# Layer B with VectorE 32x32 transposes, softmax weights normalised ahead of the value product, and column-tiled masks and sums

## The chip, the cores and the metric

The kernel runs on one core of a Trainium2 chip. The metric is the device time of one execution in microseconds (us), as a median over several runs. A core has TensorE (PE in the profile; PEld is its weight load), VectorE (DVE), ScalarE (ACT), GpSimd (POOL) and SyncE (SP), which here issues the transfers. In this program each engine executes its instructions in the order in which they are written, and waits for the others through semaphores.

## The reference, cut

Four layers, A, B, A, B, each on the layernorm of a residual stream of 2048 tokens x 640. The change touches B alone, which is recurrent: 64 segments of 32 tokens, each preceded by 8 memory rows that the segment before it has put out.

```python
def _B_ref(x, mem0, Wq, Wk, Wv, Wo, seg_len):      # H = 32 heads, Dh = 128, M = 8, seg_len = 32
    ...
    for s in range(n_seg):                          # 64 segments, one after the other
        h = concatenate([mem, x[:, s*32:(s+1)*32]]) # 8 + 32 rows
        q, k, v = h @ Wq, h @ Wk, h @ Wv
        scores = where(mask, q @ k.T * scale, -1e9)
        o = softmax(scores) @ v @ Wo
        mem = o[:, :M]                              # the next segment needs these
        outs.append(o[:, M:])
```

Two layers of 64 segments make 128 segments in a row, so a microsecond in a segment is 128 us of the total.

## The kernel before: the parts that matter

A projection ("thin" matmul) has 32 token columns as its stationary operand. Four such matmuls run side by side in the array as column tiles of 32, each with 512 columns of the weights. Q and K come out with tokens on the partitions, but the scores need the head dimension there. The kernel before evicts them to SBUF, lets TensorE transpose them (four 128x128 blocks) and scatters the result.

```python
def thin_parts(cols, Wt, b, name):
    ps = ps_tile([128, 512], F32, name)                    # one PSUM bank
    def part(c):
        for j in range(4):
            n = 4 * b + j
            nc.tensor.matmul(ps[32*j:32*j+32, :], lhsT=cols(c), rhs=Wt[:, c, 512*n:512*n+512],
                             start=(c == 0), stop=(c == NCH-1), tile_position=(0, 32*j), ...)
    return ps, [lambda c=c: part(c) for c in range(NCH)]   # NCH = 5, so 20 matmuls
def transp4(sb_half, name):
    tp = ps_tile([128, 4, 128], BF16, name)
    for i in range(4):
        nc.tensor.transpose(tp[:, i, :], sb_half[:, 128*i:128*i+128], C.identb[:])
    return tp
# ... scores(b): the mask is added by one full-array matmul of 320 columns, then 32 small column-tiled ones, then Exp
# ... sums(b): row-tiled matmuls with ones; values(b): row-tiled; both into the OTL tiles
def inverse(b, jp):                                        # 1/sum as exp(-ln(sum)), 320 columns, on ScalarE
    R = ...; nc.scalar.activation(out=R[:], in_=OTL[b, jp][:, :, 1, 0:160], func=ACT.Ln)
    nc.scalar.activation(out=R[:], in_=R[:], func=ACT.Exp, scale=-1.0)
def scale(b, jp):                                          # the heads' outputs are normalised AFTER the value product
    nc.vector.tensor_tensor(out=OTsb[...], in0=OTL[b, jp][:, :, 0, 0:160], in1=R[:], op=ALU.mult)
    for i in range(2):
        nc.gpsimd.tensor_tensor(out=Rtot[:], in0=Rtot[:], in1=R[:, i], op=ALU.add)   # range check
# ... one segment, in the order of the program:
Qa = thin_mm(cols, W.wq, 0, "b_Qa"); evac("act", Qsb[:, 0, :], Qa[:], SCB)
Ka = thin_mm(cols, W.wk, 0, "b_Ka"); evac("dve", Ksb[:, 0, :], Ka[:])
Qb = thin_mm(cols, W.wq, 1, "b_Qb"); evac("act", Qsb[:, 1, :], Qb[:], SCB)
TPQa = transp4(Qsb[:, 0, :], "b_TPQ"); scatter(...); TPKa = transp4(Ksb[:, 0, :], "b_TPK"); scatter(...)
# ... V, scores, sums, values, inverse, scale for both halves; OPS: 64 output matmuls;
# fill(): projections of later tokens ("tail") or the output pass of postponed rows ("OPSd") in TensorE's gaps
msb = ...; nc.scalar.copy(msb[:], ops[:])                  # memory rows: eviction, then six selecting matmuls (b_MT)
nc.tensor.matmul(mt[:, 0, :], lhsT=msb[:, 0:128], rhs=selm[:, 0, :], ...)                 # x6
```

PSUM, TensorE's output memory, is used up in this program: four tiles of one bank (`ps_tile`) and two of two banks (`pot`, for the heads' outputs). All engines are held to the program's order.

Of the kernel before, what the change touches and what calls it, by code (L numbers as in the profile page):

```python
# [28 lines left out]
D = 640  # L29
# [29 lines left out]
def layernorm_tile(nc, pool, C, xt, xn_out, name):  # L59
    stats = pool.tile([128, 2, nc.vector.BN_STATS_DIM], F32, name=f"{name}_st", tag="ln_st")  # L60
    nc.vector.bn_stats(out=stats[:, 0, :], in_=xt[:, 0:320])
    nc.vector.bn_stats(out=stats[:, 1, :], in_=xt[:, 320:640])
    mv = pool.tile([128, nc.vector.BN_AGGR_DIM], F32, name=f"{name}_mv", tag="ln_mv")
    nc.vector.bn_aggr(out=mv[:], in_=stats[:])
    rstd = pool.tile([128, 1], F32, name=f"{name}_rstd", tag="ln_rstd")
    nc.vector.tensor_scalar(out=rstd[:], in0=mv[:, 1:2], scalar1=LN_EPS, scalar2=None, op0=ALU.add)
    nc.gpsimd.tensor_tensor(out=rstd[:], in0=rstd[:], in1=C.mhalf[:, 0:1], op=ALU.pow)
    nc.vector.tensor_scalar(out=xn_out, in0=xt, scalar1=mv[:, 0:1], scalar2=rstd[:, 0:1],
                            op0=ALU.subtract, op1=ALU.mult)
# [496 lines left out]
def load_B_weights(nc, tc, ctx, B_Wq, B_Wk, B_Wv):  # L566
# [4 lines left out]
    for nm, src in (("wq", B_Wq), ("wk", B_Wk), ("wv", B_Wv)):  # L571
        t = wp.tile([128, NCH, 4096], BF16, name=f"b_{nm}")
        setattr(W, nm, t)
        sv = src.rearrange("(c p) h e -> p c (h e)", p=128)
        for c in range(NCH):
            loads.append(lambda t=t, sv=sv, c=c: nc.sync.dma_start(t[:, c, :], sv[:, c, :]))
# [3 lines left out]
def layer_B(nc, tc, C, W, wo_src, x_src, xb_src, x_dst, mem0, general, nsteps=64, out_bf16=False):  # L580





# [6 lines left out]
    with ExitStack() as ctx:  # L592
# [12 lines left out]
        selm = st.tile([128, 2, 8], BF16, name="b_sel")  # L605
        nc.vector.tensor_tensor(out=selm[:, 0, :], in0=C.identb[:, 24:32], in1=C.identb[:, 88:96], op=ALU.add)
        nc.vector.tensor_tensor(out=selm[:, 1, :], in0=C.identb[:, 56:64], in1=C.identb[:, 120:128], op=ALU.add)
        ones = st.tile([128, 128], BF16, name="b_ones")
        nc.vector.memset(ones[:], 1.0)
        if not general:  # L610
            Rtot = st.tile([128, 160], BF16, name="b_Rtot")
            nc.vector.memset(Rtot[:], 0.0)
        XO = st.tile([64, 320], F32, name="b_XO")
        nc.vector.memset(XO[:], 0.0)
        negs = wk.tile([128, 32], F32, name="b_negs", tag="Qsb")
        nc.vector.memset(negs[:], -1e9)
        mask = st.tile([128, 2, 40], BF16, name="b_mask")
        maskf = wk.tile([128, 2, 40], F32, name="b_maskf", tag="Ksb")
        nc.vector.memset(maskf[:], 0.0)
        for j in range(4):  # L620
            r0 = 32 * j
            nc.gpsimd.affine_select(out=maskf[r0:r0 + 24, 0, 0:24], in_=negs[r0:r0 + 24, 0:24],
                                    pattern=[[-1, 24]], compare_op=ALU.is_gt, fill=0.0, base=0, channel_multiplier=1)
            nc.vector.memset(maskf[r0:r0 + 8, 1, 0:24], -1e9)
            nc.gpsimd.affine_select(out=maskf[r0:r0 + 8, 1, 32:40], in_=negs[r0:r0 + 8, 0:8],
                                    pattern=[[-1, 8]], compare_op=ALU.is_gt, fill=0.0, base=0, channel_multiplier=1)
        nc.vector.tensor_copy(mask[:], maskf[:])
        if general:
            maskq = st.tile([128, 40], BF16, name="b_maskq")
            maskqf = wk.tile([128, 40], F32, name="b_maskqf", tag="Vsb")  # L630
# [8 lines left out]
        def evac(eng, dst, src, scale=None):  # L639
            if eng == "act":  # L640
                if scale is None:
                    nc.scalar.copy(dst, src)
                else:
                    nc.scalar.activation(out=dst, in_=src, func=ACT.Copy, scale=scale)
            else:
                if scale is None:
                    nc.vector.tensor_copy(dst, src)
                else:
                    nc.vector.tensor_scalar(out=dst, in0=src, scalar1=scale, scalar2=None, op0=ALU.mult)

# [10 lines left out]
        def ln_norm(g):  # L661
            xt = ln_x.pop(g)
            layernorm_tile(nc, sm, C, xt[:], xt[:], "b_ln")
            ln_n[g] = xt
# [33 lines left out]
        def thin_parts(cols, Wt, b, name):  # L698
            ps = ps_tile([128, 512], F32, name)

            def part(c):
                for j in range(4):
                    n = 4 * b + j
                    nc.tensor.matmul(ps[32 * j:32 * j + 32, :], lhsT=cols(c), rhs=Wt[:, c, 512 * n:512 * n + 512],
                                     start=(c == 0), stop=(c == NCH - 1), tile_position=(0, 32 * j), skip_group_check=True)
            return ps, [lambda c=c: part(c) for c in range(NCH)]

        def thin_mm(cols, Wt, b, name):
            ps, parts = thin_parts(cols, Wt, b, name)
            for f in parts:  # L710
                f()
            return ps

        def transp4(sb_half, name):
            tp = ps_tile([128, 4, 128], BF16, name)
            for i in range(4):
                nc.tensor.transpose(tp[:, i, :], sb_half[:, 128 * i:128 * i + 128], C.identb[:])
            return tp

        def scatter(eng, tp, b, dst3, t0, t1, c0):  # L720
            src = tp[:].rearrange("p i (j t) -> p i j t", j=4)[:, :, :, t0:t1]
            dst = dst3[:, 16 * b:16 * b + 16, c0:c0 + (t1 - t0)].rearrange("p (j i) c -> p i j c", j=4)
            evac(eng, dst, src)


        QTt, KTt, Vtb, Vt, tail_sb = {}, {}, {}, {}, {}
# [10 lines left out]
        class TailUnit:  # L737


            def __init__(self, T, kind, b, eng):  # L740
                self.T, self.kind, self.b, self.eng = T, kind, b, eng
                self.parts = None

            def start(self):
                Wt = {"Q": W.wq, "K": W.wk, "V": W.wv}[self.kind]
                self.ps, self.parts = thin_parts(tail_cols(self.T), Wt, self.b, "b_tail")
                if self.b == 0:
                    if self.kind == "V":
                        Vtb[self.T] = wk2.tile([128, 2, 512], BF16, name="b_Vtb", tag="Vtb")
                    else:  # L750
                        self.sb2 = tail_sb[self.kind] = wk.tile([128, 2, 512], BF16, name="b_tsb", tag="Qsb")

            def run(self, k):
# [3 lines left out]
                while k > 0 and self.parts:  # L757
                    self.parts.pop(0)()
                    k -= 1
                    if not self.parts:  # L760
                        if self.kind == "V":
                            evac(self.eng, Vtb[self.T][:, self.b, :], self.ps[:])
                        else:
                            self.sb = tail_sb[self.kind][:, self.b, :]
                            evac(self.eng, self.sb, self.ps[:], SCB if self.kind == "Q" else None)
                return k

            def transposes(self):
                if self.kind != "V":
                    self.tp = transp4(self.sb, "b_ttp")  # L770

            def finish(self):
                if self.kind != "V":
                    d = QTt if self.kind == "Q" else KTt
                    if self.b == 0:
                        d[self.T] = wk.tile([128, 32, 32], BF16, name=f"b_{self.kind}Tt", tag=f"{self.kind}Tt")
                    scatter(self.eng, self.tp, self.b, d[self.T], 0, 32, 0)
# [30 lines left out]
        def add_out(ops, XO, name):  # L808

            nc.vector.tensor_tensor(out=XO[0:64, :], in0=ops[0:64, :], in1=XO[0:64, :], op=ALU.add)  # L810
            if out_bf16:
                xnb = wk.tile([64, 320], BF16, name=name, tag=name)
# [10 lines left out]
        m0 = wk.tile([8, D], BF16, name="b_m0", tag="OTsb")  # L823
        nc.sync.dma_start(m0[:], mem0)
# [3 lines left out]
        alloc_h(0)  # L828
        mt = ps_tile([128, NCH, 8], BF16, "b_m0T")
        for c in range(NCH):  # L830
            nc.tensor.transpose(mt[:, c, :], m0[0:8, 128 * c:128 * c + 128], C.identb[0:8, 0:8])
        nc.vector.tensor_copy(hT[0][:, :, 24:32], mt[:])
        alloc_qk(0)
        for kind in ("Q", "K", "V"):
            for b in range(2):
                u = TailUnit(0, kind, b, ("act", "dve")[b])
                u.run(NCH)
                u.transposes()
                u.finish()
        for nm, Wt, sc, dst in (("Q", W.wq, SCB, QT), ("K", W.wk, None, KT)):  # L840
            for b in range(2):
                ps = thin_mm(lambda c: hT[0][:, c, 0:32], Wt, b, "b_first")
                sb = wk.tile([128, 512], BF16, name="b_fsb", tag=("Qsb", "Ksb")[b])
                evac(("act", "dve")[b], sb[:], ps[:], sc)
                scatter(("act", "dve")[b], transp4(sb, "b_ttp"), b, heads(dst[0]), 0, 24, 0)
# [14 lines left out]
        for s in range(nsteps):  # L860
# [12 lines left out]
            elif T + 1 < NT:  # L873
                kind = " VQK"[i4]
                units = [TailUnit(T + 1, kind, 0, "act"), TailUnit(T + 1, kind, 1, "dve")]
# [8 lines left out]
            for u in units:  # L884
                if isinstance(u, TailUnit) and u.kind != "V":
                    queue.append((0.31, lambda u=u: (u.transposes(), u.finish())))
# [10 lines left out]
            Qsb = wk.tile([128, 2, 512], BF16, name="b_Qsb", tag="Qsb")  # L897
            Ksb = wk.tile([128, 2, 512], BF16, name="b_Ksb", tag="Ksb")
            Vsb = wk.tile([128, 2, 512], BF16, name="b_Vsb", tag="Vsb")
            PT = wk.tile([128, 2, 2, 4, 40], BF16, name="b_PT", tag="PT")  # L900
# [4 lines left out]
            mrows = []  # L905

            def row_max(b):
# [20 lines left out]
                mr = wk.tile([3, 16, 40], BF16, name="b_mrows", tag="mrows")  # L928
# [3 lines left out]

            def scores(b):
                sp = ps_tile([128, 2, 4, 40], F32, "b_SP")
                nc.tensor.matmul(sp[:], lhsT=C.identb[:], rhs=mask[:].unsqueeze(2).to_broadcast([128, 2, 4, 40]),
                                 start=True, stop=False, skip_group_check=True)
                for r in range(4):
                    for k, n in ((0, 32), (1, 8)):
                        for j in range(4):
                            h = 16 * b + 4 * j + r  # L940
                            nc.tensor.matmul(sp[32 * j:32 * j + n, k, r, :], lhsT=KT[s][:, 40 * h + 32 * k:40 * h + 32 * k + n],
                                             rhs=QT[s][:, 40 * h:40 * h + 40], start=False, stop=True,
                                             tile_position=(0, 32 * j), skip_group_check=True)
                if general:
                    for k, n in ((0, 32), (1, 8)):
                        for j in range(4):
                            h = 4 * j
                            nc.tensor.matmul(sp[32 * j:32 * j + n, k, :, :], lhsT=ones[0:3, 0:n], rhs=mrows[b][:, h:h + 4, :],
                                             start=False, stop=True, tile_position=(0, 32 * j), skip_group_check=True)
                acc = {} if general else {"accum_out": seen[:, b:b + 1]}  # L950
                nc.scalar.activation(out=PT[:, b], in_=sp[:], func=ACT.Exp, **acc)

            def ot(b, j):
                return OTL[b, j // 2][:, j % 2]

            def sums(b):

                for jp in range(2):
                    OTL[b, jp] = pot.tile([128, 2, 2, 256], F32, name="b_OTL", tag="ot")
                for k, n in ((0, 32), (1, 8)):  # L960
# [247 lines left out]
```

## Time and profile before

| | before |
|---|---|
| time, median of the three runs at hand | 3002.18 us |
| segments of B, mean of 63 starts in each layer | 17.3 us |
| TensorE busy in the first layer B | 93% |
| VectorE / ScalarE / GpSimd busy there | 44 / 48 / 33% |

How to read it: "busy" is the time in which an engine has an instruction under way; the granted clock (PEclk) is a share of TensorE's full speed. The chain of waits is followed back from the last instruction, at each step to what released it. An engine that is 93% busy and fills the chain is the bound, and idle time of the others costs nothing.

The windows view of the kernel before, for a stretch in the first layer B; columns are microseconds, then busy time and count for each engine, clock, share of DMA and GB/s:

```profile
...
core 0: us, PE busy (x) PEld busy (x) DVE busy (x) ACT busy (x) POOL busy (x), PEclk, DMA share, GB/s
400.00:1480.00 1080.00, 1008.75 (x25097) 548.72 (x25101) 472.56 (x1112) 522.58 (x1340) 360.96 (x900) 1.00 0.08 18
...
```

1008.75 of 1080 us is the 93%. One segment in the chain of waits of the kernel before (start us, us, engine and tile):

```profile
...
1007.61 1.19 PE b_Qa L86 x20
1008.80 1.08 PE b_Ka L86 x20
1009.88 1.08 PE b_Qb L86 x20
1010.96 0.33 PE b_TPQ L86 x4
1011.29 0.22 PE b_TPK L86 x4
1011.52 1.19 PE b_V L86 x20
1012.71 0.55 PE b_SP L86 x33
1013.26 1.12 PE b_Kb L86 x20
...
1023.15 0.46 PE b_MT L86 x6
...
```

The projections follow each other every 1.08 us. The transposes (b_TPQ, b_TPK) stand in the chain with 0.33 and 0.22 us.

### The profile page before, as it was taken

The numbers are of one execution on the slowest core, as the hardware profiler recorded it, in microseconds if no ns is written. First come the engines' busy times: TensorE is split into PE (matmuls) and PEld (weight loads), VectorE is DVE, ScalarE is ACT, GpSimd is POOL, SyncE is SP. The second block draws the span as 40 slices with busy tenths as digits, with TensorE's granted clock in tenths as the row PEclk, the third lists the DMA queues.
The fourth block names the chain that finished last, engine by engine and source line by source line (L and its number), as shares of the span: only waits on it lengthen the run. The fifth ranks groups of instructions, "written<-read, shape, count | busy, mean of one in ns | idle before, by whom it ended". The sixth has DMA issues, their size and how long they took to land.

```text
span 2998.1 us, 129696 instructions
## 1 busy us (share of the span) xinstructions
PE 2659.2 (89%) x57506; PEld 1431.5 (48%) x57568; DVE 1408.6 (47%) x3411; ACT 1487.9 (50%) x3315; POOL 998.8 (33%) x2465
## 2 busy tenths in 40 slices
PE   6888789999999999999778886899999999999997
PEld 3444345555555555555434443455555555555554
DVE  4666444444444444444456663444444444444443
ACT  4666444444444444444356663444444444444443
POOL 2343323333333333333323442333333333333332
PEclk9988799999999999999978897999999999999999
DMA  7422400000000000000123333000000000000000
GB/s 267 133 90 76 138 19 18 19 18 20 20 18 19 19 18 18 19 18 16 27 88 111 111 96 129 14 17 16 17 17 17 17 17 15 17 17 18 14 14 12
DMA packets 98156, 132.24 MB, mean 44 GB/s; under 512 B 19872, under 2 KB 83376, under 8 KB 95664
## 3 DMA queue, kind: packets, MB, share of 16 engines
q1 hardware_dynamic: 95984, 122.19, 14.0%
q8 instruction: 452, 7.41, 1.0%
q10 hardware_dynamic: 1600, 1.66, 0.2%
q14 instruction: 120, 0.98, 0.1%
HBM read 89.17 MB, written 26.21 MB: 38 GB/s over the span
## 4 chain that ended last, share of the span: by engine, by line
PE 61%; DVE 9%; ACT 8%; issue 7%; POOL 6%; DMA 1%; SPq 0%; POOLq 0%; DVEq 0%; ACTq 0%
PE b_V L86 10%; PE b_Qa L86 5%; PE b_Kb L86 5%; PE b_Ka L86 5%; POOL b_Rtot L86 5%; ACT b_R L86 5%; PE b_Qb L86 5%; PE b_SP L86 5%; PE b_OPS L86 4%; PE b_tail L86 4%; PE b_TPQ L86 3%; PE a_PP L86 2%; PE b_TPK L86 2%; DVE b_OTsb L86 2%; PE b_OTL L86 2%
## 5 line engine op out<-in xcount | busy, mean ns | idle before, releaser
L86 POOL TENSOR_TENSOR b_Rtot<-b_Rtot,b_R 128x160 bf16<-128x160 bf16 x1024 | 502.9, 491 | 1347.8 <-ACT b_R L86 1287.6
L86 PEld LDWEIGHTS <-b_hT 128*32 128x32 bf16 x15520 | 389.9, 96 | 314.6 <-POOL b_KT L86 9.2
L86 DVE TENSOR_TENSOR b_OTsb<-b_OTL,b_R 128x320 bf16<-128x320 f32 x512 | 250.4, 489 | 338.3 <-ACT b_R L86 335.2
L86 PE MATMUL b_OPS<-b_wo,b_OTsb 128*32 128x320 bf16 x8192 | 347.8, 301 | 59.4 <-DVE b_OTsb L86 58.6
L86 ACT ACTIVATE b_R<-b_OTL 128x320 f32<-128x320 f32 x512 | 219.7, 429 | 294.2 <-POOL b_Rtot L86 236.1
L86 ACT ACTIVATE a_PT<-a_S 128x768 bf16<-128x768 f32 (+1 forms) x384 | 325.7, 891 | 80.4 <-PE a_S L86 72.0
L86 PE MATMUL b_V<-b_wv,b_hT 128*32 128x512 bf16 x5120 | 348.4, 382 | 0.0
L86 PEld LDWEIGHTS <-b_OTsb 128*32 128x32 bf16 x8192 | 191.6, 96 | 171.0 <-DVE b_OTsb L86 124.5
L86 ACT ACTIVATE b_R<-b_R 128x320 f32<-128x320 f32 x512 | 241.2, 471 | 16.3
L86 DVE CAST b_Ksb<-b_Kb 128x512 bf16<-128x512 f32 x128 | 88.5, 692 | 304.1 <-PE b_Kb L86 304.1
L86 DVE COPY b_KT<-b_TPK 128x128 bf16<-128x128 bf16 x508 | 123.9, 286 | 139.0 <-PE b_TPK L86 139.0
L86 POOL TENSOR_SCALAR_AFFINE_SELECT a_PT<-a_PT 128x256 bf16<-128x256 bf16 x256 | 109.8, 433 | 212.3 <-ACT a_PT L86 197.7
L86 ACT ACTIVATE b_Qsb<-b_Qb 128x512 bf16<-128x512 f32 x128 | 76.5, 597 | 198.6 <-PE b_Qb L86 198.6
L86 ACT ACTIVATE b_Qsb<-b_Qa 128x512 bf16<-128x512 f32 x128 | 76.5, 597 | 185.4 <-PE b_Qa L86 183.6
L86 PE MATMUL b_Qa<-b_wq,b_hT 128*32 128x512 bf16 x2560 | 164.1, 385 | 3.3 <-DVE b_hT L86 2.2
L86 PE MATMUL b_Kb<-b_wk,b_hT 128*32 128x512 bf16 x2560 | 163.2, 380 | 0.0
L86 PE MATMUL b_Ka<-b_wk,b_hT 128*32 128x512 bf16 x2560 | 163.1, 383 | 0.0
L86 PE MATMUL b_Qb<-b_wq,b_hT 128*32 128x512 bf16 x2560 | 160.8, 379 | 0.0
L86 PE MATMUL b_OTL<-b_PT,b_ones 32*128 32x160 bf16 (+1 forms) x2048 | 111.6, 234 | 54.2 <-DVE b_OTsb L86 52.4
L86 ACT COPY b_QT<-b_TPQ 128x128 bf16<-128x128 bf16 (+1 forms) x382 | 115.7, 340 | 84.4 <-PE b_TPQ L86 84.4
L86 PE MATMUL a_PP<-a_xnT,a_wt 128*128 128x512 bf16 x505 | 148.5, 408 | 9.2 <-issue 5.5
L86 PE MATMUL a_S<-a_qk 32*128 32x512 bf16 (+3 forms) x1024 | 143.2, 321 | 7.1 <-ACT a_PT L86 5.8
(181 smaller groups left out, 4336.5 us busy)
## 6 DMA issues: line engine op xcount, KB each, us to landing
a_wt<-a_wpad SPq DMA_DIRECT2D x112, 160.0 KB
b_wo<-in_B_Wo_dram SPq DMA_DIRECT2D x8, 1280.0 KB
b_Vt<-b_Vtb SPq DMA_DIRECT2D x512, 16.0 KB
b_XO<-xres SPq DMA_DIRECT2D x256, 30.0 KB
a_wvo<-in_A_wo_dram SPq DMA_DIRECT2D x8, 800.0 KB
b_wq<-in_B_Wq_dram SPq DMA_DIRECT2D x5, 1024.0 KB
b_wk<-in_B_Wk_dram SPq DMA_DIRECT2D x5, 1024.0 KB
b_wv<-in_B_Wv_dram SPq DMA_DIRECT2D x5, 1024.0 KB
```

The costliest lines, as they stand in the source:

```text
L86: r = f(*a, **k)
```

## The change

Its intent is to take work off TensorE and to shorten the waits:

- Q and K are not transposed by TensorE any more. The weights are read in an order in which VectorE's transpose, which turns each 32x32 block by itself, leaves each head where the scores need it. VectorE reads PSUM (fp32, 128x512) and writes SBUF; VectorE and GpSimd place the columns. The 8 memory rows take the same way, so the selecting matmuls (b_MT) go.
- The softmax weights are normalised ahead of the value product, on 160 columns.
- Mask and sums are column-tiled, in the same tiling as the projections and scores.
- The PSUM tiles are dealt out anew: Q and K of one half share a two-bank tile from the pool of the heads' outputs.

The core of the diff, cut:

```diff
-        def transp4(sb_half, name):
-            tp = ps_tile([128, 4, 128], BF16, name)
-            for i in range(4):
-                nc.tensor.transpose(tp[:, i, :], sb_half[:, 128 * i:128 * i + 128], C.identb[:])
...
+        def pair_tile(name):
+            return pot.tile([128, 2, 512], F32, name=name, tag="ot")
...
+        def w_heads(Wt, c, b, j):
+            return Wt[:, c, :].rearrange("p (b h j e) -> p b j h e", b=2, h=16, j=4)[:, b, j]
...
+        def turn(ps):
+            tq = wk2.tile([128, 16, 32], F32, name="b_TQ", tag="TQ")
+            nc.vector.transpose(out=tq[:].rearrange("p h t -> p (h t)"), in_=ps)
+            return tq
...
+            def qk(Wt, ps, b, dst):
+                thin_mm(ps, cols, Wt, b, w_heads)
+                tq = turn(ps)
+                place("dve", tq, b, heads(dst[s]), 0, 8, 24)
+                if not last:
+                    place("pool", tq, b, heads(dst[s + 1]), 8, 32, 0)
...
+                for j in range(4):     # mask, column-tiled
+                    nc.tensor.matmul(sp[32 * j:32 * j + 32, :, 0:40], lhsT=C.identb[:, 32 * j:32 * j + 32], ...
...
+            def normalise(b):
+                nc.scalar.activation(out=R[:], in_=SP[b][:, 256:416], func=ACT.Ln)
+                nc.scalar.activation(out=R[:], in_=R[:], func=ACT.Exp, scale=-1.0)
+                nc.vector.tensor_tensor(out=PT[:, b, :, 16:56], in0=PT[:, b, :, 16:56], in1=Rv, op=ALU.mult)
+                nc.vector.tensor_tensor(out=PT[:, b, :, 0:16], in0=PT[:, b, :, 0:16], in1=Rv[:, :, 24:40], op=ALU.mult)
+                    nc.gpsimd.tensor_tensor(out=Rtot[:], in0=Rtot[:], in1=R[:], op=ALU.add)
...
+            A_, B_ = pair_tile("b_QKa"), pair_tile("b_QKb")
+            qk(W.wq, A_[:, 0, :], 0, QT)
+            qk(W.wk, A_[:, 1, :], 0, KT)
+            qk(W.wq, B_[:, 0, :], 1, QT)
+            scores(0)
+            qk(W.wk, B_[:, 1, :], 1, KT)
...
-                xnb = wk.tile([64, 320], BF16, name=name, tag=name)
+                xnb = wk.tile([64, 320], BF16, name=name, tag="xnb")
...
-                mt = ps_tile([128, NCH, 8], F32, "b_MT")
-                nc.tensor.matmul(mt[:, 0, :], lhsT=msb[:, 0:128], rhs=selm[:, 0, :], start=True, stop=True)
+                TM = wk.tile([128, 10, 32], F32, name="b_TM", tag="TM")
+                nc.vector.transpose(out=TM[:].rearrange("p g t -> p (g t)"), in_=ops[:])
```

## The prediction

> **What bounds it.** The span is 2998 us. The two layers B are the stretches 383 to 1487 and 1878 to 2983 us (chain of waits, in order of time): 64 segments of 17.3 us each, 128 x 17.3 = 2210 us. In 400:1480 TensorE is busy 93% at granted clock 1.00, VectorE 44%, ScalarE 48%, GpSimd 33% (windows), and the chain runs mostly through TensorE: TensorE bounds, plus a few in-order waits. One segment of the chain (1007.6 to 1024.4, 16.8 us): six projections of 1.08 to 1.24 us; transposes of Q and K 0.33+0.22+0.33+0.37 = 1.25; scores with mask 2 x 0.55; sums and values about 0.5 each; 64 output matmuls 2.3; filler 2.2; memory-row selection (MT) 0.46. Between 1017.4 and 1021.05 the chain leaves TensorE: GpSimd Rtot, then Ln 0.45, Exp 0.48, scaling 0.50, although TensorE fills much of that time.
>
> The four kinds of segment take 16.8, 16.5, 17.9, 18.0 us. The last two carry tail transposes: VectorE eviction 0.70, transposes 0.40, wait about 1.1 us; the third also a layernorm ahead of them.
>
> **Removed, per segment (TensorE).** Transposes 1.25; tail transposes and their waits, about 1.1 in every second segment, 0.6 on average; MT 0.46 and the wait for its eviction (0.43 on ScalarE); mask matmul of 320 full-array columns (0.135 at the projections' rate) becomes four concurrent ones of 160 (0.07); sums likewise, about 0.15 each. Tiling switches: the Trainium skill (TensorEngine Tiling (Array Packing), Key Properties) says a change of tiling mode drains TensorE; the trace agrees: twenty V matmuls after a transpose cost 1.19, without one 1.08. About 16 switches fall to 4: 1 us or more, partly counted already. My TensorE sum falls from 15.3 to 12.3 us. The scaling behind 1017.4 goes: normalising waits for Ln and Exp of 160 columns, hidden under V projections. GpSimd's Rtot drops from 8 to 2 adds of 0.49.
>
> **Added.** Four VectorE transposes of 128x512 fp32 from PSUM. The skill (VectorE: DVE Perf Modes, The three transpose paths) gives 311 ns for 128 columns; the trace has 0.69 us for a 128x512 cast, so I estimate 0.70 each. They replace two such casts and scatters. With placings (0.22), V evictions, normalising, memory row (0.5+2x0.2), residual adds: VectorE about 10 us of 13.5, against 7.6 of 17.3. The memory chain (about 1.4 us after the last output matmul) is covered by 1.3 to 1.5 us filler. After Q and K tail segments and the deferred output pass, VectorE starts late (tail transposes 0.70, adds 0.98), so scores wait 0.4 to 0.7 us; a layernorm ahead of the memory transpose costs about 1 us every fourth segment. Mean: 12.5 + 0.45 + 0.25, plus 0.5 for VectorE/GpSimd collisions and switches: 13.75 us.
>
> **Sum.** 128 x (17.26 - 13.75) = 449; two prologues (tails at 352 to 383 us wait for evictions and transposes) 12 each: 24. Layer A unchanged. 3002 - 473 = **2529 us**, range 2430 to 2670. Faster by over 2%: 0.96; within 2%: 0.03; slower: 0.01.
>
> **Right if:** segments of 13.2 to 14.2 us; no TensorE transposes in B except layernorm's; Q/K projection groups still 1.08 us; VectorE transposes near 0.70; GpSimd Rtot gone from the chain; VectorE 70 to 75% in B; chain mostly TensorE, with VectorE at segment joins.
>
> **Wrong if:** Q/K weights read in strided runs of 32 columns slow the matmuls (each 10% adds 0.43 us per segment, 55 us in all); the fp32 transpose takes far over 0.7 us, making VectorE the bound (1.2 us each would add 2 us of VectorE per segment); VectorE's SBUF-to-SBUF ops block against GpSimd's placings; the shorter segment exposes memory chain or V-row DMA.

## The result, and the profile after

The changed kernel takes 2796.35 us (median of 4 runs, 2793.6 to 2799.32), against 3003.47 us for the kernel before beside it. The ratio is 0.9314, with a 95% interval of 0.9301 to 0.9328. Here and below a ratio is the mean time of one kernel's fast runs over that of the other's of the same rounds, so it is not quite the ratio of the medians quoted. It is 6.9% faster, where about 16% was predicted; 2796 lies outside the stated range of 2430 to 2670.

| | before | after | predicted |
|---|---|---|---|
| time (median beside each other) | 3003.47 | 2796.35 | 2529 |
| us a segment, first / second layer B | 17.28 / 17.30 | 15.71 / 16.16 | 13.75 |
| PE busy, whole span (us) | 2659.2 | 2327.0 | |
| VectorE busy, whole span (us) | 1408.6 | 1753.7 | |

A segment's time is the distance from the start of the first Q projection of a layer to the start of its last one, divided by 63. 15.71 and 16.16 are 1.96 and 2.41 us above the predicted 13.75; times 64 each that is 280 us, so the whole miss of 267 us lies in the segments (about 13 us came back elsewhere). The windows view of the changed kernel:

```profile
...
core 0: us, PE busy (x) PEld busy (x) DVE busy (x) ACT busy (x) POOL busy (x), PEclk, DMA share, GB/s
360.00:1380.00 1020.00, 872.79 (x24547) 491.85 (x24535) 658.90 (x1452) 236.59 (x753) 368.77 (x857) 0.99 0.10 23
...
```

TensorE is busy 872.79 of 1020 us, 86%, down from 93%. It had less to do, as predicted, but it also stood still more. VectorE is at 65%. So TensorE waits for something. The beginning of a segment in the chain of waits of the changed kernel:

```profile
...
1032.94 1.17 PE b_QKa L87 x20
...
1034.20 0.73 DVE b_TQ L87
...
1034.97 1.26 PE b_QKa L87 x20
1036.23 1.10 PE b_QKb L87 x20
...
1037.43 0.73 DVE b_TQ L87
...
1038.20 1.26 PE b_QKb L87 x20
...
1039.56 1.08 PE b_V L87 x20
...
```

Q of the first half, then VectorE's transpose, and only then K of the first half; the same again in the second half. In the kernel before these projections ran back to back. But K does not need Q's transpose: K is another product of the same inputs. The timeline of TensorE alone shows the wait (start us, us, engine, line, operation, and in brackets the idle time before it and who ended it):

```profile
...
1032.82 1.26 PE L87 MATMUL b_QKa<-b_wq,b_hT 128*32 128x512 bf16 x20
1034.97 1.26 PE L87 MATMUL b_QKa<-b_wk,b_hT 128*32 128x512 bf16 x20 [0.89 <-DVE b_TQ L87]
1036.05 1.27 PE L87 MATMUL b_QKb<-b_wq,b_hT 128*32 128x512 bf16 x20
...
```

and that of VectorE shows what it waited for:

```profile
...
1032.70 1.01 DVE L87 TENSOR_TENSOR b_XO<-b_OPS,b_XO 64x320 f32<-64x320 f32 x2
1034.20 0.72 DVE L87 STREAM_TRANSPOSE b_TQ<-b_QKa 128x512 f32<-128x512 f32 x1 [0.49 <-PE b_QKa L87]
1034.95 0.23 DVE L87 CAST b_QT<-b_TQ 128x128 bf16<-128x128 f32 x1
1036.35 0.72 DVE L87 STREAM_TRANSPOSE b_TQ<-b_QKa 128x512 f32<-128x512 f32 x1 [1.17 <-PE b_QKa L87]
...
```

The first transpose ends at 1034.92, and K starts at 1034.97. The next projection, Qb into the other tile, starts at 1036.05 and runs on while VectorE reads K out of the first tile from 1036.35. The list of waits of TensorE in the changed kernel (total us, times, longest us) adds them up:

```profile
...
PE b_QKa L87 <- DVE b_TQ L87: 192.2, 128, 3.6
PE b_QKb L87 <- DVE b_TQ L87: 50.2, 128, 1.0
PE b_QKa L87 <- DVE b_hT L87: 32.3, 34, 1.2
...
```

128 waits in front of each of the two K projections, one a segment: 192 + 50 = 242 us. (In the tile b_QKb the Q projection came first, so its wait is that of the second K.) What Q and K share is the PSUM tile: `A_[:, 0, :]` and `A_[:, 1, :]` are two banks of one tile. The Trainium skill (Perfetto Trace Analysis, Matmuls) advises to rotate independent groups through different PSUM banks so that the eviction of one overlaps the matmuls of the next. This program did put Q and K into different banks, and the trace shows no overlap. Nor is it the memory that makes the second access slow: in all 128 segments K's first matmul carries a wait for VectorE's semaphore, which the framework put there, and Qb's first matmul carries none.

### The profile page after: what moved, and what is told of

Read it like the earlier page. It is cut to its first block, busy times and chain, and to the rows that moved or that the text cites. A ratio compares the mean times of both kernels' runs of the same rounds, so it can differ in the third digit from the quotient of the medians.

```text
span 2796.9 us, 123979 instructions
## 1 busy us (share of the span) xinstructions
PE 2327.0 (83%) x54988; PEld 1285.9 (46%) x54988; DVE 1753.7 (63%) x4029; ACT 882.6 (32%) x2067; POOL 994.4 (36%) x2333
## 4 chain that ended last, share of the span: by engine, by line
PE 55%; DVE 19%; issue 7%; ACT 5%; DMA 2%; SPq 1%; POOL 1%; DVEq 0%; ACTq 0%; POOLq 0%
PE b_QKb L87 11%; PE b_V L87 10%; DVE b_TQ L87 9%; PE b_OPS L87 9%; PE b_QKa L87 8%; PE b_tail L87 3%; PE a_PP L87 3%; PE b_SP L87 3%; ACT a_PT L87 2%; PE b_OTL L87 2%; ACT b_OTsb L87 1%; PE a_S L87 1%; DVE b_TM L87 1%; ACT b_R L87 1%; DVE b_XO L87 1%
## 5 line engine op out<-in xcount | busy, mean ns | idle before, releaser
L87 PE MATMUL b_QKa<-b_wk,b_hT 128*32 128x512 bf16 x2560 | 179.9, 413 | 192.2 <-DVE b_TQ L87 192.2
L87 DVE STREAM_TRANSPOSE b_TQ<-b_QKa 128x512 f32<-128x512 f32 x256 | 183.5, 717 | 193.3 <-PE b_QKa L87 190.6
L87 DVE STREAM_TRANSPOSE b_TQ<-b_QKb 128x512 f32<-128x512 f32 x256 | 183.5, 717 | 175.2 <-PE b_SP L87 116.0
L87 DVE TENSOR_TENSOR b_PT<-b_PT,b_R 128x160 bf16<-128x160 bf16 (+1 forms) x512 | 215.0, 460 | 44.8 <-ACT b_R L87 44.4
L87 POOL TENSOR_TENSOR b_Rtot<-b_Rtot,b_R 128x160 bf16<-128x160 bf16 x256 | 142.8, 558 | 240.1 <-ACT b_R L87 224.5
L87 PE MATMUL b_QKb<-b_wk,b_hT 128*32 128x512 bf16 x2560 | 161.6, 380 | 50.2 <-DVE b_TQ L87 50.2
L87 PE MATMUL b_QKa<-b_wq,b_hT 128*32 128x512 bf16 x2560 | 162.9, 381 | 32.4 <-DVE b_hT L87 32.3
L87 ACT CAST b_OTsb<-b_OTL 128x320 bf16<-128x320 f32 x384 | 148.7, 421 | 114.5 <-PE b_OTL L87 114.4
L87 DVE CAST b_Vsb<-b_V 128x512 bf16<-128x512 f32 x256 | 174.4, 684 | 7.4 <-PE b_V L87 6.4
L87 PE MATMUL b_QKb<-b_wq,b_hT 128*32 128x512 bf16 x2560 | 175.0, 402 | 0.0
```

What stands on the lines that cost most here:

```text
L87: r = f(*a, **k)
```

## The experiments

Theory A: the wait comes from the shared tile. The framework that inserts the semaphores treats a write to one bank of a tile as a conflict with a read of the other, so K waits until VectorE has read Q. Theory B: VectorE is the bound in effect; it is busier and comes late (residual additions and tail transposes stand ahead of Q's transpose), and without the shared tile TensorE would wait one step later, at the scores. Unless it says otherwise, each edit below is made on the changed kernel, whose time is 2796.

### e1_own_bank: K in a tile of its own

```diff
-            qk(W.wk, A_[:, 1, :], 0, KT)
+            qk(W.wk, ps_tile([128, 512], F32, "b_Ka")[:], 0, KT)
...
-            qk(W.wk, B_[:, 1, :], 1, KT)
+            qk(W.wk, ps_tile([128, 512], F32, "b_Kb")[:], 1, KT)
```

> Edit on the changed kernel: only the two K projections move into single-bank PSUM tiles of their own, so a K projection no longer shares a tile with the Q projection whose transpose VectorE is reading; order and work of all engines stay. Theory A (the wait is made by the shared pair tile: idle before the K projections 192 + 50 us, plus about 0.18 us of restart in each of 256 groups): the idle of TensorE before b_QKa and b_QKb on the transposes goes to about 0 and the time falls by 180 to 260 us, to 2540 to 2615 us. Theory B (VectorE itself is late or overloaded, so the wait would only move to the scores that need its result): the wait moves to b_SP and the time stays above 2735 us.

Measured: 2555.73 us, ratio to before 0.8514 (0.8500 to 0.8528), results correct. That is 241 us less than the changed kernel, from two lines. Its waits:

```profile
...
PE b_SP L87 <- DVE b_KT L87: 70.8, 90, 2.6
PE b_QKa L87 <- DVE b_hT L87: 31.8, 34, 1.2
...
```

No wait of a projection for a transpose is left. Some of it did move on to the scores, 71 us, as theory B has it, but not the bulk. VectorE is now at 72% (653.50 of 908 us in the first layer B), higher than before the edit, and the kernel is faster. A segment takes 13.83 us in the first layer B and 14.28 in the second.

A second cost went with the wait. In the changed kernel the group with the longest waits also ran slower:

```profile
...
L87 PE MATMUL b_QKa<-b_wk,b_hT 128*32 128x512 bf16 x2560 | 179.9, 413 | 192.2 <-DVE b_TQ L87 192.2
L87 PE MATMUL b_QKb<-b_wq,b_hT 128*32 128x512 bf16 x2560 | 175.0, 402 | 0.0
...
```

413 and 402 ns mean, with single matmuls up to 634 ns, against 379 ns as the usual value. In the segment at 1051 us, K came after a wait of 1.63 us that followed a layernorm's, and its 20 matmuls took 2.33 us instead of 1.26; the windows view gives a granted clock of 0.50 from 1051.45 to 1053.50. In e1 the same groups average 383 and 380 ns. The traces tie the slow matmuls to the granted clock: of 687 projection matmuls above 450 ns in the changed kernel, 673 started while the recorded clock was 0.5, and e1 has 175 slow ones in all. Within 4 us they followed 15 of the 19 stops of more than 2 us in layer B, but only 13 of 106 stops of 0.9 to 2 us. What makes the clock fall was not tested.

The gain of e1 can be added up. The waits fall by 242 - 71 = 171 us. The rest is my estimate: a projection that follows a stop stands in the chain with 1.26 us instead of 1.08, 256 x 0.18 = 46 us; 512 fewer slow matmuls at (2.33 - 1.26) / 20 us each are 27 us. Together 244 us, against 241 measured.

### e2_cross_tiles: same two tiles, other partners

```diff
-            qk(W.wk, A_[:, 1, :], 0, KT)
-            qk(W.wq, B_[:, 0, :], 1, QT)
+            qk(W.wk, B_[:, 0, :], 0, KT)
+            qk(W.wq, A_[:, 1, :], 1, QT)
```

> Edit on the changed kernel: same two pair tiles, but Qa and Qb share the one and Ka and Kb the other, so each projection shares with the one before the last; no bank added. Theory A: Ka no longer waits, Qb waits for a transpose that has had one more group (1.08 us) of time, so most of the gain of e1 is there: 2560 to 2650 us. Theory B: above 2735 us.

Measured: 2556.16 us, ratio 0.8510 (0.8496 to 0.8524), as good as e1 and 4 us below the range that theory A expected; theory B falls. No bank was added, no work moved; a projection now shares its tile with the one before the last, whose transpose has had 1.08 us more to finish. The wait that is left is still on the tile's partner (here Qb, which is named b_QKa because it lies in the first tile):

```profile
...
PE b_QKa L87 <- DVE b_TQ L87: 61.3, 90, 2.5
...
```

61 us in 90 waits, where e1 has 71 us at the scores: the same lateness of VectorE, seen at another place. e1 and e2 together show that the partner in the tile makes the wait. That the tracking goes by whole tile, and not by neighbouring banks, the two runs do not separate. The changed kernel itself does: in all 128 segments Qb's projection runs, without a wait, while VectorE reads K out of the other tile. The trace gives no bank numbers, but the built program does: in one of the two layers B the first tile has banks 4 and 5, the second 6 and 7. So there Qb is written into bank 6 while VectorE reads its neighbour 5, and K, written into bank 5, waits for the read of bank 4.

### e3_late_residual: VectorE's order alone

The residual additions and stores of a segment are put behind the third transpose of the next one (the row store becomes a function in a list `late`, which runs after `scores(0)`; the store of postponed rows and the load of the next residual rows move with it).

```diff
+            while late:
+                late.pop(0)()
...
-            xo = add_out(ops, XO, "b_xnb")
+            def store_rows(s=s, ops=ops):
+                xo = add_out(ops, XO, "b_xnb")
...
+            late.append(store_rows)
```

> Edit on the changed kernel: the residual additions and stores of a segment move on VectorE from ahead of the first Q transpose of the next segment to after its third transpose; shared tiles stay. Theory A: the K projection still waits for a transpose of 0.72 us that starts as soon as Qa ends; only the part of the 1.5 us mean idle beyond 0.85 us goes, 50 to 100 us: 2700 to 2750 us. Theory B (VectorE's order makes the wait): nearly all of the 242 us goes, 2560 to 2610 us.

Measured: 2749.88 us, ratio 0.9164 (0.9149 to 0.9180), 46 us less; at the edge of theory A's range and far from B's. The wait before the first K falls to what the transpose itself takes:

```profile
...
PE b_QKa L87 <- DVE b_TQ L87: 113.8, 128, 0.9
PE b_QKb L87 <- DVE b_TQ L87: 45.8, 128, 0.5
...
```

113.8 us over 128 segments is 0.89 us, near the 0.72 us of the transpose plus two hand-overs. So VectorE's order made the wait longer, but the shared tile made it a wait. These two waits fell by 83 us and the time by only 46, partly because a new one came up: the scores now wait for b_KT, 44.6 us in 31 waits (0.4 us before). In the longest of them the moved additions stand ahead of the last K transpose on VectorE, and themselves wait for the store that e4 deals with.

### e4_own_output_tile: the second layer B

In the last layer two output tiles, of the segment's rows and of the postponed rows, had got the same buffer.

```diff
-                xnb = wk.tile([64, 320], BF16, name=name, tag="xnb")
+                xnb = wk.tile([64, 320], BF16, name=name, tag="xnb" if name == "b_xnb" else "xn")
```

> Edit on the changed kernel: in the last layer the deferred rows' bf16 output tile no longer shares its buffer with the segment's output tile (it takes the layernorm output's buffer, idle at that time). In the trace of the changed kernel the second layer B takes about 16.1 us a segment against 15.7 in the first, and DMA stores of that tile stand in its chain. If the shared buffer causes it, the time falls by 20 to 30 us (2766 to 2776 us), all in the second layer B; if not, it is within 5 us of the changed kernel's 2796.

Measured: 2766.87 us, ratio 0.9214 (0.9199 to 0.9230), 29.5 us less. A segment of the second layer B falls from 16.16 to 15.75 us; the first stays at 15.71. VectorE's timeline of the changed kernel, where it stood still:

```profile
...
2736.20 0.49 DVE L87 TENSOR_TENSOR b_xnb<-b_OPS,b_XO 64x320 bf16<-64x320 f32 x1
2736.73 0.48 DVE L87 TENSOR_TENSOR b_XOd<-b_OPSd,b_XOd 64x320 f32<-64x320 f32 x1
2738.58 0.49 DVE L87 TENSOR_TENSOR b_xnbd<-b_OPSd,b_XOd 64x320 bf16<-64x320 f32 x1 [1.37 <-DMA out_dram<-b_xnb]
2739.11 0.72 DVE L87 STREAM_TRANSPOSE b_TQ<-b_QKa 128x512 f32<-128x512 f32 x1
...
```

The addition into b_xnbd waited 1.37 us for the store of b_xnb, out of the same buffer, and the transpose that TensorE was waiting for stood behind it. So this cost, too, reached TensorE mostly through the wait for the shared tile, which in e4 is 21 us shorter than the 192.2 us of the changed kernel:

```profile
...
PE b_QKa L87 <- DVE b_TQ L87: 171.1, 128, 1.7
...
```

A separate tag of its own did not fit into SBUF (a build failed by 0.56 KB a partition), so the edit borrows the buffer of the layernorm's output, which is idle at that time.

### e7_no_inverse_sum: do VectorE and GpSimd collide?

GpSimd's sum of the inverses is left out (the range check is then blind to them; the output is the same).

```diff
-                if not general:
-                    nc.gpsimd.tensor_tensor(out=Rtot[:], in0=Rtot[:], in1=R[:], op=ALU.add)
```

> The changed kernel without GpSimd's running sum of the inverses (the range check is then blind to them; the output is the same). Collision theory: VectorE's two normalising products (0.44 and 0.48 us; the 64-column one takes longer than the 160-column one) are held by GpSimd's sum that reads SBUF at the same time; without it they fall to about 0.32 and 0.22. Rival: that is their own duration, and they stay. Either way little of it is on the path: the time falls by 0 to 40 us.

Measured: 2795.41 us, ratio 0.9312, no change in time. The two normalising products in the changed kernel, and then without the sum:

```profile
...
L87 DVE TENSOR_TENSOR b_PT<-b_PT,b_R 128x64 bf16<-128x64 bf16 x256 | 123.3, 482 | 0.0
L87 DVE TENSOR_TENSOR b_PT<-b_PT,b_R 128x160 bf16<-128x160 bf16 x256 | 112.3, 439 | 44.8 <-ACT b_R L87 44.4
...
```

```profile
...
L87 DVE TENSOR_TENSOR b_PT<-b_PT,b_R 128x160 bf16<-128x160 bf16 x256 | 112.6, 440 | 37.0 <-ACT b_R L87 19.0
...
L87 DVE TENSOR_TENSOR b_PT<-b_PT,b_R 128x64 bf16<-128x64 bf16 x256 | 72.0, 281 | 0.0
...
```

The 64-column product falls from 482 to 281 ns, the mean of the 160-column one stays at 440. But that mean mixes two cases. The timeline without the sum shows the 160-column product in the first and in the second half of one segment:

```profile
...
1032.35 0.56 POOL L87 CAST b_KT<-b_TQ 128x384 bf16<-128x384 f32 x1 [1.59 <-DVE b_TQ L87]
...
1032.46 0.62 DVE L87 TENSOR_TENSOR b_PT<-b_PT,b_R 128x160 bf16<-128x160 bf16 x1
...
1034.96 0.32 DVE L87 TENSOR_TENSOR b_PT<-b_PT,b_R 128x160 bf16<-128x160 bf16 x1
...
```

The first started while GpSimd was placing K, the second with GpSimd idle. Over this whole trace the 98 products that start during such a placing take 625 ns on average and the other 158 take 325; in the changed kernel it is 622 and 325. GpSimd's sum is never under way when this product starts, so leaving it out could not help. The 64-column product takes 218 ns with no GpSimd instruction under way at its start, 512 behind the sum, and 332 or 411 behind GpSimd's copies. So the collision theory holds for both products; only the partner of the 160-column one was not the sum. The Trainium skill (SBUF — State Buffer, Who interferes with whom) says that a VectorE instruction with two SBUF inputs contends with a GpSimd instruction that reads SBUF; both products agree. That 0.2 us twice a segment changes nothing in the total shows how little this part of VectorE's busy time counted in the changed kernel; in e9, where the scores wait for VectorE, it was not tried.

### e8_before_column_mask: one part of the change alone, on the kernel before

```diff
-                nc.tensor.matmul(sp[:], lhsT=C.identb[:], rhs=mask[:].unsqueeze(2).to_broadcast([128, 2, 4, 40]),
-                                 start=True, stop=False, skip_group_check=True)
+                for j in range(4):
+                    nc.tensor.matmul(sp[32 * j:32 * j + 32, :, :, :], lhsT=C.identb[:, 32 * j:32 * j + 32],
+                                     rhs=mask[:].unsqueeze(2).to_broadcast([128, 2, 4, 40]),
+                                     start=True, stop=False, tile_position=(0, 32 * j), skip_group_check=True)
```

> One part of the change alone, on the kernel before: the mask is added by four column-tiled matmuls of the same 320 columns in place of one full-array matmul; the columns streamed stay the same. If a change of tiling mode costs about 0.1 us of TensorE each (two fewer in each of 256 score groups): the time falls by 40 to 60 us, to 2940 to 2960 us. If changes of mode cost nothing here: within 8 us of the kernel before.

Measured: 2953.14 us, ratio 0.9839 (0.9822 to 0.9855), 48 us less than before, with the same columns streamed. That is 1.6%, under the 2% from which a run is called faster, but its interval lies clear of 1. TensorE's timeline of the kernel before, from the V projection over the mask to the scores, and then with the column-tiled mask:

```profile
...
1011.45 1.26 PE L86 MATMUL b_V<-b_wv,b_hT 128*32 128x512 bf16 x20
1012.64 0.31 PE L86 MATMUL b_SP<-b_mask,c_identb 128*128 128x320 bf16 x1
1012.88 0.38 PE L86 MATMUL b_SP<-b_QT,b_KT 128*32 128x40 bf16 x32
...
```

```profile
...
1000.75 1.26 PE L86 MATMUL b_V<-b_wv,b_hT 128*32 128x512 bf16 x20
1001.84 0.31 PE L86 MATMUL b_SP<-b_mask,c_identb 128*32 128x320 bf16 x4
1001.98 0.40 PE L86 MATMUL b_SP<-b_QT,b_KT 128*32 128x40 bf16 x32
...
```

From start to start, V to mask falls from 1.19 to 1.09 us, and mask to scores from 0.24 to 0.14: 0.10 us for each change of tiling mode (the means over all 128 groups behind a V projection are the same). Two in each of 256 score groups make 512 x 0.10 = 51 us, near the 48 measured. The Trainium skill (TensorEngine Tiling (Array Packing), Key Properties) states that a change of tiling mode drains TensorE, without a figure; this run shows what a change costs. The weight loads fit it: before, the mask's weights were loaded at 1012.64, together with the mask matmul; column-tiled they were loaded at 1001.63, 0.21 us ahead of it and under the V matmuls.

### e5, e6 and e9: what is left after e1

The remaining waits were the scores' for VectorE, and the layernorm (b_hT, 32 us). e6 splits the layernorm so that its last operation stands behind the memory transpose; e5 is e1, e3, e4 and that split together; e9 is e1 and e4 alone.

```diff
-                ln_norm(g_need)
+                ln_apply = ln_norm(g_need, split=True)     # statistics here, the last operation below
...
+            if ln_apply is not None:                       # after the transpose and additions of the memory rows
+                ln_apply()
```

> The changed kernel with four edits at once: K projections in banks of their own (e1), late residual additions (e3), own output buffer (e4), and the layernorm split so that its statistics stay ahead of the transpose of the memory rows and its last operation goes behind it (e6). Expected if the gains are of separate waits: e1's 2556 us, less about 25 (output buffer), less most of the 71 us that the scores still wait for VectorE, less 40 to 80 (layernorm): 2400 to 2470 us. If VectorE (72% busy in layer B of e1) already bounds, the three further edits only move its work: above 2500 us.

> e1's edit with the layernorm split alone. The layernorm's operations (2 x 0.48, 0.22, 0.17, then 0.56 on GpSimd, 0.65) stand ahead of the memory transpose in 32 of 128 segments and hold back the next segment by about 2 us, after which TensorE's matmuls run at half speed for a while. If that is the cost: 40 to 90 us less than e1, 2465 to 2515 us. If other waits cover it: above 2540 us.

> e1's banks plus e4's output buffer, nothing else. In e5 the first layer B took 13.9 us a segment against e1's 13.8, so the residual and layernorm moves seem to have gained nothing and the 21 us of e5 to be the output buffer's alone. Then this kernel takes e1's 2556 less 25 to 30: 2524 to 2534 us, no slower than e5. If those moves did gain, it is slower than e5 by 10 us or more.

Measured: e5 2534.79 us (ratio 0.8446, 0.8432 to 0.8460), e6 2547.99 (0.8491, 0.8477 to 0.8505), e9 2533.14 (0.8434, 0.8423 to 0.8446). Two misses: e5 and e6 gained far less than the range expected first; for both the second case that the expectation named came true. In e6 the wait for b_hT falls from 31.8 to 7.1 us, but that of the scores for b_KT rises from 70.8 to 83.7: the edit moved VectorE's work and mostly moved the wait along. e9, without the two reorderings, is as fast as e5. So the split and the late additions are worth nothing together with e1 and e4, and e9 is the version to keep: 13.83 and 13.94 us a segment, 9.4% below the changed kernel (0.8434 / 0.9314 = 0.906). TensorE is busy 757.27 of 800 us from 400 to 1200 us in it, 95%.

### e10 and e11: giving ScalarE the V evictions

```diff
-            evac("dve", Vsb[:, 0, :], Va[:])
+            evac("act", Vsb[:, 0, :], Va[:])
```

(and the same for the second half; e10 on e9, e11 on e5.)

> e9 with the two V evictions (0.68 us each, both on VectorE) moved to ScalarE, which is 26% busy in layer B of e1 while VectorE is 72% busy. If VectorE's queue still sets part of the segment (scores and normalising wait for it), the time falls by 20 to 60 us, 2465 to 2510 us. If TensorE alone bounds what is left, it stays within 10 us of e9.

> e5 with the V evictions on ScalarE: with VectorE unloaded, the late residual additions and the split layernorm should no longer collide with its work in the middle of the segment. Expected 10 to 40 us below e10 if those moves are worth anything once VectorE has room: 2440 to 2490 us; at e10's time or above if they are not.

Measured: e10 2568.83 us (0.8553, 0.8541 to 0.8564) and e11 2576.31 (0.8577, 0.8566 to 0.8589), both slower than e9. e10 missed both of its cases; e11 came out as its second case has it, at e10's time or above, far from the range that it named first. The output matmuls' wait in e9 and then in e10:

```profile
...
PE b_OPS L87 <- ACT b_OTsb L87: 13.1, 39, 0.9
...
```

```profile
...
PE b_OPS L87 <- ACT b_OTsb L87: 61.3, 128, 1.2
PE b_SP L87 <- DVE b_KT L87: 49.8, 91, 0.8
...
```

The second V eviction (0.59 us) now stands on ScalarE ahead of the logarithm of the second half and of the evictions that the output matmuls need, and their wait grows from 13 to 61 us. The wait for b_KT, which the edit was meant to shorten, stays at 49.8. ScalarE was little used on average, but at that point it was on the path.

## Why the prediction was wrong, point by point

**The step that failed** is the sum for a segment in "Added": "Mean: 12.5 + 0.45 + 0.25, plus 0.5 for VectorE/GpSimd collisions and switches: 13.75 us." Its 12.5 us let the projections Qa, Ka, Qb and Kb run back to back, and let VectorE be late only for the scores ("so scores wait 0.4 to 0.7 us"). The diff shows that Q and K share a tile, and the prediction did not ask what else that tile orders. The runs showed a wait of TensorE in front of each K projection, 242 us in all, plus the restarts and slow matmuls after it. Giving K a tile of its own (e1) takes away 241 of the 267 us that were missing, and re-pairing the tiles (e2) does the same. That is shown.

**The second missing term** is the shared output buffer in the last layer, one changed word in the diff, 29.5 us (e4) in the changed kernel and 23 us on top of e1 (2555.73 to 2533.14), where the scores' wait falls by 21 us (70.8 to 49.8). With both mended the kernel takes 2533 us (e9) against the predicted 2529. That the two agree within 4 us is partly luck: the segments are still 0.08 and 0.19 us longer than 13.75, 17 us in all, and 13 us came back elsewhere.

**Right:** the transposes cost what was estimated (b_TQ 717 ns for 128x512 fp32 out of PSUM, predicted 0.70). Weights read in runs of 32 columns do not slow the matmuls: in e1 the Q and K groups average 380 to 383 ns, V's contiguous ones 380. Changes of tiling mode cost 0.10 us each (e8). TensorE's share of the work fell. From the layernorm's statistics to the first Q projection, the prologue of the first layer B took 35.8 us before (347.5 to 383.3) and 21.3 after (349.9 to 371.2), 14.5 saved where 12 were predicted.

**Wrong but small:** "a layernorm ahead of the memory transpose costs about 1 us every fourth segment" sounded removable; once e1 was in, removing it gave only 8 us (e6). The normalising products took 0.44 and 0.48 us, twice a segment, and the prediction had not costed them one by one; e7, which took off 0.2 us of each pair, changed nothing in the changed kernel. Collisions were in its sum with "0.5 for VectorE/GpSimd collisions and switches", which no run measures as a total; one of its risks under "Wrong if", that VectorE's SBUF-to-SBUF operations block against GpSimd's placings, came true in 98 of the 256 160-column products, 0.3 us each. VectorE was forecast at 70 to 75% in layer B: it was at 65%, since TensorE's stops stretched the segment, and at 72% in e1.

**Left open:** what makes the granted clock fall after some stops and not after others; and whether a finer order on VectorE could take back the 50 us that the scores still wait for it in e9.

## What to carry to other kernels

Two independent results in two banks of one PSUM tile can be as dependent, in a framework like this one, as if they lay in one bank: before packing them together, ask who reads the one while the other is being written, and if it must be packed, pair results whose readers are far apart (e2 cost nothing). The same goes for a shared SBUF buffer whose last reader is a store. When a big change falls short, look in the list of waits of the busiest engine for a release that the data do not need; a mean busy share of another engine (here VectorE at 65 to 72%) is a weak reason, and so is an idle one (ScalarE in e10). And before a mean duration is taken as an instruction's own, look whether it mixes two cases (e7).

## What the Trainium skill lacked or had wrong

- VectorE: DVE Perf Modes (The three transpose paths) has a figure for the VectorE transpose of 128x128 bf16 alone, 311 ns. The runs add fp32 from PSUM to SBUF: 717 ns for 128x512, 514 ns for 128x320.
- TensorEngine Tiling (Array Packing) (Key Properties) gives no size for the drain at a change of tiling mode. e8 shows 0.10 us for each, 48 us for 512 of them.
- Perfetto Trace Analysis (Matmuls) advises different PSUM banks for independent groups. In the changed kernel different banks did not help, because both lay in one tile: 242 us of waits, gone with tiles of their own (e1, 241 us faster). I found no page that names this trap.
- SBUF — State Buffer (Who interferes with whom) agrees with both normalising products, but gives no time for such a pair. The runs show 325 ns with no GpSimd instruction under way and 622 to 625 behind GpSimd's placing of K (160 columns), and 218 ns against 512 behind GpSimd's sum (64 columns).
